# Denominators, softmax sums and gates spread by VectorE's 32x32 transposes instead of small transfers and broadcasts, phi(k) sums by additions, and another order

## The chip, the cores and the metric

The kernel runs on one core of one Trainium2 chip. The metric is the device time of one execution in microseconds. A profiled execution is taken beside the timed ones; its span runs from the first to the last instruction.

## The reference

Inputs are q, k and v of 8 batches x 8 heads x 576 positions x 64, and the weights. First comes linear attention, whose output, heads side by side, is the input x (576 x 512 per batch) of four causal attention experts of which each position uses two:

```python
def phi(x):
    proj = np.einsum('bhsd,df->bhsf', x, w_phi)
    proj = proj - np.max(np.abs(proj), axis=-1, keepdims=True)
    return np.concatenate([np.exp(proj), np.exp(-proj)], axis=-1)
q_p, k_p = (phi(q), phi(k))
kv = np.einsum('bhsf,bhsd->bhfd', k_p, v)
z = np.sum(k_p, axis=2)
num = np.einsum('bhsf,bhfd->bhsd', q_p, kv)
den = np.einsum('bhsf,bhf->bhs', q_p, z)[..., None] + 1e-06
x = num / den
...
logits = x @ w_gate          # gates: the 2 best of 4 experts, softmax over them
for e in range(4):
    q, k, v = x @ wq[e], x @ wk[e], x @ wv[e]
    a = causal_softmax(0.125 * (q @ k.T))
    out += gate[e] * (a @ v @ wo[e])
```

## The kernel before

**Staging.** Work goes by pairs of heads p (32 in all, four per batch) and, per batch b, by groups g of two experts (n = 2b+g, 16 in all). For a pair: `stream_k` projects k, `center` takes the maximum and subtracts it, ScalarE takes both exponentials into `ek`; `key_sum` sums `ek` over four blocks of positions into `zs` (28 of the 32 pairs); `stream_kv` multiplies `ek` with v and with ones and brings the result into `kv`. `stream_q` and `phi_q` do the same for q, with the maximum over partitions taken by GpSimd (`partition_all_reduce`), and leave the two halves of phi(q) in `mx` and `u`.

**Denominators.** `stream_n` computes a pair's denominators in two parts of positions (L633). `evac_d` copies them out of PSUM into rows of `dr`; four small transfers bring a row into 64 partitions x 9 numbers (`dc`), VectorE adds and inverts these (L665, L668), two transfers bring them back as rows, and GpSimd broadcasts the rows to the partitions of `xf` (L675, L677). Then the numerators (L643) are multiplied by `xf` in `divide` (L683), and the product is split into a high and a low part, xh and xl.

**Experts.** `stream_b` projects q and k of a group (`proj_t`), v and the gate logits of a batch (`proj_v`), then takes scores. `gates` computes the gate weights on VectorE (L822 to L840) into `gw` (the tile named col), transposes them on TensorE (L845) and sends them to DRAM. `mask` and `maxima` mask the scores and take the maximum over keys (GpSimd again, L885), L889 subtracts it, `expo` exponentiates. `sums` adds over keys with a matrix of ones (L919), copies the rows out into `max`, moves them by transfers to 64 x 9 (`sc`), inverts them, multiplies them with the gates read back from DRAM, moves them back and broadcasts them into `rb` (L947, L949). `attend` multiplies with v (L976), `evac_y` scales by `rb` (L988) and splits into yh and yl, `project_out` applies wo and `evac_o` stores.

**Order.** All DMAs are issued from SyncE's queue. The program order on each engine is fixed: a planner (`Plan`) runs the generators above as streams with a rank each (`POS`, `POS1`, `BOFF`, `NPOS`, `SLOPE`), estimates when each next step could start from written-down costs, and issues the step of best rank among those that can start soonest; copies out of PSUM go to ScalarE or VectorE by the same estimate. `in_order` then pins that order. TensorE works in three tilings (128x128, 64x128 and 128x32); eight PSUM tiles `c` are shared by all streams. Buffer counts: one `dr` (`DB`), one `rb` (`RB`), two `max` (`MB`).

Of the kernel before, what the change touches and what calls it, by code (L numbers as in the profile page):

```python
# [33 lines left out]
MB = 2  # L34
SUMJ = ()
SPLIT = 396
CACT = ()
TAILPE = True
RB = 1
DB = 1  # L40
PXB = 5
HOT = 1.08
SLOPE = (-6.05, 0.45, 3.02, 1.24, 1.41)
NPOS = (-8.38, 1.08)
UB = 4
FLEX = (5, -193)
# [5 lines left out]
ZEROS = 1.45  # L52

POS1 = {'k': -2.07, 'q': -0.65, 'v': 0.13, 'kv': 0.14, 'z': 0.36, 'cen': 0.7, 'evu': -4.26, 'ph0': 1.44, 'ph1': 0.38, 'div': 3.37, 'evd': -1.16, 'lk': -2.12, 'lq': -0.19}
BOFF = (0.83, 1.78, 1.5, 1.79, 1.95, 0.61, 1.44, 1.24)

ORDER = (('p0', 'v0', 's0', 'p1', 's1'), ('p0', 's0', 'p1', 's1', 'v0'))
POS = {'p0': 6.37, 'p1': -3.26, 'v0': 8.55, 'gate': 5.43, 's0': -1.94, 's1': 2.49, 'm0': 3.33, 'm1': 5.61, 't0': 5.6, 't1': 8.79, 'out': 13.84}
NPAIRS = B * NP
HEAD = 0.17  # L60
# [6 lines left out]
OTHER = 2.52  # L67
# [172 lines left out]
def tile_linear_attn_moe(ctx, tc, qt, kt, v, wts, out):  # L240
# [104 lines left out]
    drs = [sb(f"dr{i}", [128, S]) for i in range(DB)]  # L345
    dc = [sb(f"dc{i}", [128, 3, 9]) for i in range(2)]
# [6 lines left out]
    scs = [sb(f"sc{g}", [128, 9]) for g in range(2)]  # L353
# [118 lines left out]
    def key_sum(p, ek, ekk):  # L472
        for c in range(2):
            yield Step('DVE', ekk, pred=has('kv', p - 1) if p else None)
            dve(1024, ['zs'], ekk).tensor_reduce(out=zs[:, c], in_=ek[:, c, 0:8, :].rearrange("p (h a) f -> p h f a", h=2), axis=AX.X, op=ALU.add)  # L475
# [37 lines left out]
    def stream_kv():  # L513


        for p in range(NPAIRS):
# [6 lines left out]
            for t in range(NJ):  # L523
                for h in range(2):
                    u_ = 4 * h + t if t < 4 else 8
                    for k in range(2):
                        g = slice(64 * h + 32 * k, 64 * h + 32 * k + 32)
                        plan.run('PE', 256 / TRATE + 2, [kc], ekk + [vk], tiling=(128, 32))
                        nc.tensor.matmul(o[g, 0:2], v_in[:, 4 * h + t if t < 4 else 8 + h, 32 * k:32 * k + 32], ek[:, :, u_, :].rearrange("p c (w f) -> p c w f", w=4),  # L529
# [83 lines left out]
    def stream_n():  # L613


        for p in range(NPAIRS):
# [5 lines left out]
            def ready():  # L622
                return (all(('phi', p, h) in done for h in range(2)) and ('kvs', p) in done
                        and (p < DB or ('rb', p - DB) in done))

            for s0, s1 in PARTS:
                pk, ps = yield Step('PE', Pk + [kvk], 'c', ready, tiling=(128, 32)), rank(p) + NPOS[0]
                n = s1 - s0
                for h in range(2):
                    for c in range(2):  # L630
                        g = 64 * h + 32 * c
                        plan.run('PE', n / TRATE + 2, [pk], Pk + [kvk], tiling=(128, 32))
                        nc.tensor.matmul(ps[g:g + 32, 0:n], kvi[:, g // 32, 64:96], P_[h][c][:, s0:s1],  # L633
                                         start=True, stop=True, skip_group_check=True)
                plan.spawn(evac_d(p, s0, s1, pk, ps), rank(p) + POS1['evd'])
            for s0, s1 in PARTS:
                pk, ps = yield Step('PE', Pk + [kvk], 'c', has('rb', p), tiling=(128, 32)), rank(p) + NPOS[1]
                n = s1 - s0
                for c in range(2):
                    for h in range(2):  # L640
                        for g in range(64 * h, 64 * h + 64, 32):
# [6 lines left out]
    def evac_d(p, s0, s1, pk, ps):  # L648
# [6 lines left out]
        if not all(('dr', p, q_[0]) in done for q_ in PARTS):  # L655
            return
# [437 lines left out]
```

## Time and profile before

| | |
|---|---|
| median of 3 runs | 724.03 us (722.28 to 724.15) |
| the profiled execution's own time | 725.42 us |
| its span | 723.6 us |
| mean granted clock of TensorE | 0.964 |
| TensorE, VectorE, ScalarE, GpSimd busy | 663.6, 600.5, 399.8, 338.4 us |
| partition all-reduces of GpSimd (L604, L885) | 141.8 and 57.4 us |
| its four broadcast lines (L675, L677, L947, L949) | 30.9, 31.7, 14.1, 14.6 us |

Busy time is the union of an engine's instructions. A timeline row gives start, duration, engine, line, operation and count, and in brackets the idle time ahead and what ended it. A group's row gives busy time, mean duration in ns, and the idle time just before its members. A float32 matmul leaves two records, so counts of the trace are twice those of the program there.

### The profile page before, as it was taken

To read this page: it belongs to the slowest core of one execution; us is meant where nothing else is said; L and a number is where in the kernel's file an instruction comes from. 1 tells how busy PE (TensorE), PEld (TensorE's weight loads), DVE (VectorE), ACT (ScalarE), POOL (GpSimd) and SP (SyncE) were. 2 spreads that over 40 slices of the span, in tenths; PEclk is the share of its full clock that TensorE was granted. 3 is DMA by queue.
4 is the path that set the end of the run, shared out by engine and by line. 5 is a ranking of instruction groups with operands and counts; after the bars stand their busy time and mean duration, and the time that the engine had idled before them with its cause. 6 is when DMAs were issued, how large, how long until landed. Compare 5 with 4: busy or idle time off the path is not lost.

```text
span 723.6 us, 20271 instructions
## 1 busy us (share of the span) xinstructions
PE 663.6 (92%) x8058; PEld 505.2 (70%) x8058; DVE 600.5 (83%) x1155; ACT 399.8 (55%) x797; POOL 338.4 (47%) x263
## 2 busy tenths in 40 slices
PE   8989998899989999889988999998999899989984
PEld 6755668576786668555777777865787576858874
DVE  6888998979987889888998998897999985774742
ACT  4866656455756556435665755644576462463432
POOL 4635346643445554274336643375636631452420
PEclk9999999989999999999999999899999999999997
DMA  7642431123512152132421233222430221110011
GB/s 203 160 124 75 133 95 46 34 71 83 141 41 70 31 143 56 45 119 49 118 82 40 66 110 88 72 61 74 119 85 3 75 76 25 41 52 3 2 68 67
DMA packets 67007, 55.12 MB, mean 76 GB/s; under 512 B 43584, under 2 KB 49888, under 8 KB 66912
## 3 DMA queue, kind: packets, MB, share of 16 engines
q1 hardware_dynamic: 66912, 53.82, 27.0%
q8 instruction: 64, 1.05, 0.6%
q14 instruction: 31, 0.25, 0.1%
HBM read 38.16 MB, written 15.02 MB: 73 GB/s over the span
## 4 chain that ended last, share of the span: by engine, by line
PE 41%; DVE 24%; DMA 11%; SPq 9%; issue 8%; ACT 5%; POOL 2%; DVEq 0%; POOLq 0%; ACTq 0%
PE ps_c L265 13%; SPq L297 9%; PE ps_c L529 5%; PE ps_c L643 4%; PE ps_c L919 4%; PE ps_c L442 4%; DVE zs L475 4%; PE ps_c L770 4%; PE ps_c L976 3%; DMA dc<-dr 3%; PE ps_c L633 2%; DVE top L881 2%; DVE ek L502 2%; DMA ot<-in_wts_dram 2%; DVE pmax L488 2%
## 5 line engine op out<-in xcount | busy, mean ns | idle before, releaser
L604 POOL PARTITION_ALL_REDUCE mx<-u x64 | 141.8, 2258 | 115.9 <-ACT u L274 99.0
L475 DVE TENSOR_REDUCE zs<-ek 128x256 f32<-128x1024 f32 x56 | 110.3, 1986 | 3.5 <-PE ps_c L545 2.1
L265 PE MATMUL ps_c<-xh,qk 128*128 128x320 f32 (+1 forms) x512 | 108.7, 304 | 0.2
L276 ACT ACTIVATE ek<-ek 128x1152 f32<-128x1152 f32 x64 | 74.7, 1167 | 31.3 <-DVE ek L502 30.3
L265 PEld LDWEIGHTS ps_c<-xh,qk 128*128 128x128 f32 x512 | 85.1, 193 | 1.8 <-issue 0.6
L529 PE MATMUL ps_c<-ek,v_in 128*32 128x256 f32 x1280 | 80.9, 398 | 3.3 <-ACT ek L276 1.8
L868 POOL TENSOR_SCALAR_AFFINE_SELECT s<-s 128x256 f32<-128x256 f32 (+1 forms) x80 | 49.6, 652 | 71.3 <-ACT s L274 32.6
L885 POOL PARTITION_ALL_REDUCE max<-top x16 | 57.4, 3589 | 50.2 <-DVE top L881 15.0
L265 PE MATMUL ps_c<-xl,qk 128*128 128x256 f32 (+1 forms) x256 | 76.9, 300 | 0.6 <-DVE xl L269 0.6
L889 DVE TENSOR_TENSOR s<-s,max 128x1152 f32<-128x1152 f32 (+4 forms) x80 | 73.6, 955 | 1.1 <-POOL max L885 1.1
L276 ACT ACTIVATE s<-s 128x1152 f32<-128x1152 f32 (+4 forms) x80 | 55.5, 747 | 20.7 <-DVE s L889 19.5
L529 PEld LDWEIGHTS ps_c<-ek,v_in 128*32 128x32 f32 x1280 | 43.0, 114 | 33.6 <-issue 4.9
L265 PE MATMUL ps_c<-yh,wo 128*128 128x256 f32 (+1 forms) x256 | 56.6, 316 | 9.3 <-ACT yh L274 7.2
L675 POOL PARTITION_BROADCAST xf<-dr x32 | 30.9, 966 | 70.7 <-DMA dr<-dc 47.7
L265 PE MATMUL ps_c<-vg,xh 128*128 128x260 f32 (+1 forms) x320 | 59.8, 287 | 2.0 <-DVE rb L988 1.4
L442 PE MATMUL ps_c<-q_in,wf 64*128 64x256 f32 (+1 forms) x256 | 46.4, 434 | 10.7 <-ACT u L274 4.8
L606 DVE TENSOR_TENSOR u<-u,mx 128x576 f32<-128x576 f32 x64 | 53.5, 840 | 1.0 <-POOL mx L604 0.9
L276 ACT ACTIVATE mx<-u 128x576 f32<-128x576 f32 x64 | 43.6, 682 | 18.6 <-DVE u L606 18.4
L265 PEld LDWEIGHTS ps_c<-yh,wo 128*128 128x128 f32 x256 | 43.3, 201 | 13.2 <-ACT yh L274 7.5
L488 DVE TENSOR_REDUCE pmax<-ps_c 128x4 f32<-128x512 f32 (+1 forms) x96 | 50.2, 544 | 2.2 <-PE ps_c L442 2.2
L919 PE MATMUL ps_c<-s,ones 128*32 128x180 f32 (+5 forms) x576 | 48.7, 342 | 3.5 <-ACT s L276 2.9
L502 DVE TENSOR_TENSOR ek<-ps_c,pmax 128x512 f32<-128x512 f32 (+1 forms) x96 | 51.0, 547 | 0.1
(128 smaller groups left out, 1566.0 us busy)
## 6 DMA issues: line engine op xcount, KB each, us to landing
v_in<-in_v_dram SPq DMA_DIRECT2D x32, 320.0 KB
q_in<-in_qt_dram SPq DMA_DIRECT2D x64, 144.0 KB
out_dram<-ot SPq DMA_DIRECT2D x32, 288.0 KB
kvd<-kvt SPq DMA_DIRECT2D x112, 48.0 KB
kv<-kvd SPq DMA_DIRECT2D x28, 192.0 KB
k_in<-in_kt_dram SPq DMA_DIRECT2D x32, 160.0 KB
k_in<-in_kt_dram SPq DMA_DIRECT2D x32, 128.0 KB
dc<-dr SPq DMA_DIRECT2D x128, 2.2 KB
```

The lines of the kernel that those rows point to most:

```text
L265: nc.tensor.matmul(o, a, b, start=start, stop=stop, skip_group_check=True)
L276: nc.scalar.activation(o, i, func, **kw)
L297: nc.sync.dma_start(o, i)
L442: nc.tensor.matmul(o, a, b, start=True, stop=True, skip_group_check=True)
L475: dve(1024, ['zs'], ekk).tensor_reduce(out=zs[:, c], in_=ek[:, c, 0:8, :].rearrange("p (h a) f -> p h f a", h=2), axis=AX.X, op=ALU.add)
L488: dve(n * 128, [mk], [pk]).tensor_reduce(out=m[:, us], in_=src, axis=AX.X, op=ALU.max, apply_absolute_value=True)
L502: dve(n * 128, [e1k], [pk, mk]).tensor_tensor(out=ek2[p % EKB][:, 1, us, :], in0=src, in1=m[:, us].unsqueeze(2).to_broadcast([128, n, 128] ...
L529: nc.tensor.matmul(o[g, 0:2], v_in[:, 4 * h + t if t < 4 else 8 + h, 32 * k:32 * k + 32], ek[:, :, u_, :].rearrange("p c (w f) -> p c w f" ...
L604: nc.gpsimd.partition_all_reduce(M, U, 128, bass_isa.ReduceOp.absmax)
L885: nc.gpsimd.partition_all_reduce(big.rearrange("p e s -> p (e s)"), top.rearrange("p e s -> p (e s)"), 128, bass_isa.ReduceOp.max)
L889: dve(2 * (S - 128 * j), [('d', x, j)], [('max', z)], port=True).tensor_tensor(out=block(s_, j), in0=block(s_, j), in1=big[:, :, 128 * j:S ...
L919: nc.tensor.matmul(ps[r:r + 32, a - lo:z - lo], ones, src[:, e, a - c0:z - c0], start=first, stop=k == len(mine) - 1, skip_group_check=True)
```

## The change

In `key_sum`, two reductions per pair become three additions. In `stream_n` the two parts of the denominators become one PSUM tile of 32 equal rows per quarter: head h and every other block of 32 positions go to partitions 64*half + 32*h. The new helper `fractions` serves denominators and softmax sums: a 32x32-block transpose out of PSUM puts 32 positions on 32 partitions, so 9 columns hold all; these are inverted (and, for the sums, multiplied with the gates), copied to the other half of the partitions, widened to 576 columns and transposed again, which spreads each position's number over 32 partitions. `gates` no longer goes through DRAM: 16 small matmuls with pieces of the identity place the weights in `gc`. To fit the partitions, the columns of v, `vs` and the rows of the weights are taken in steps of two, and each weight piece is loaded in two halves. `dr`, `dc`, `sc`, `gtr`, `gd`, the 328 small transfers and 96 broadcasts are gone; `rb` gets two buffers, `max` one. The ranks and some of the planner's costs are other numbers, so every engine's order changes.

```diff
-MB = 2
-SUMJ = ()
-SPLIT = 396
+MB = 1
+NX = 1
-RB = 1
-DB = 1
+RB = 2
-NPOS = (-8.38, 1.08)
+NPOS = (-7.5, 3.69)
...
     def key_sum(p, ek, ekk):
-        for c in range(2):
-            yield Step('DVE', ekk, pred=has('kv', p - 1) if p else None)
-            dve(1024, ['zs'], ekk).tensor_reduce(out=zs[:, c], in_=ek[:, c, 0:8, :].rearrange("p (h a) f -> p h f a", h=2), axis=AX.X, op=ALU.add)
+        x = ek[:, :, 0:8, :].rearrange("p c (h a) f -> p c h a f", h=2)
+        for a in range(1, 4):
+            yield Step('DVE', ekk, pred=has('kv', p - 1) if p else None, port=True)
+            dve(512, ['zs'], ekk, 1.11, True).tensor_tensor(out=zs, in0=zs if a > 1 else x[:, :, :, 0], in1=x[:, :, :, a], op=ALU.add)
...
-    def evac_d(p, s0, s1, pk, ps):
...
+    def fractions(a, n, ps, pk, eps, out, wk, free, flag, gate=None):
+        i = n % NX
+        X, C, both = spreads[a][i]
+        key, bk = f'wide{a}{i}', f'both{a}{i}'
+        yield Step('DVE', [pk], pred=has('wide', a, n - NX) if n >= NX else None, hot=True)
+        dve(S // 2, [key], [pk], 1.13).transpose(X[:, 0:S // 2], ps[:, 0:S // 2])
+        plan.release('c', (pk, ps))
+        yield Step('DVE', [key], hot=True)
+        dve(9, [bk], [key]).tensor_scalar(out=C, in0=X[:, 0:S // 2:32], scalar1=eps, scalar2=None, op0=ALU.add)
+        halves = [(0, 0), (1, 1), (0, 1), (1, 0)]
+        if gate is None:
+            for src, dst in halves:
+                r, w = slice(64 * src, 64 * src + 64), slice(64 * dst, 64 * dst + 64)
+                yield Step('DVE', [bk], hot=True)
+                if src == dst:
+                    dve(9, [bk], [], 6.0).reciprocal(both[w, :, src], C[r])
+                else:
+                    dve(9, [bk], []).tensor_copy(both[w, :, src], both[r, :, src])
+        else:
+            yield Step('DVE', [bk], hot=True)
+            dve(9, [bk], [], 6.0).reciprocal(C, C)
+            for src, dst in halves:
+                r, w = slice(64 * src, 64 * src + 64), slice(64 * dst, 64 * dst + 64)
+                yield Step('DVE', [bk, 'gc'], pred=has('gate', n // 2), hot=True)
+                dve(9, [bk], ['gc']).tensor_tensor(out=both[w, :, src], in0=C[r], in1=gate[r], op=ALU.mult)
+            done.add(('gated', n))
+        st = Step((('ACT', 95 + 0.83 * S), ('DVE', 65 + 1.04 * S)), [bk], hot=True)
         yield st
+        copy(st.eng, S, X.rearrange("p (t i) -> p t i", i=32), both.rearrange("p a b -> p (a b)").unsqueeze(2).to_broadcast([128, 18, 32]), [key], [bk])
+        yield Step('DVE', [key], pred=free, hot=True)
+        dve(S, wk, [key], 1.13).transpose(out, X)
+        done.update((('wide', a, n), flag))
...
     def gates(b):
...
-        kc, ps = yield Step('PE', [G], 'c')
-        plan.run('PE', LDW, [kc], [G])
-        nc.tensor.transpose(ps[:, 0:128], gw, ident)
...
+        for g in range(2):
+            for a in range(2):
+                for half in range(2):
+                    for e in range(2):
+                        r, c = 64 * half + 32 * e, 64 * a + 32 * half
+                        nc.tensor.matmul(o[r:r + 32, g, :, a], ident[:, c:c + 32], gw[:, 5 * (2 * g + e):5 * (2 * g + e) + 5], start=True, stop=True, skip_group_check=True)
...
     def sums(n):
...
+        for j in range(NJ):
+            src = block(s_, j).rearrange("p e (a b i) -> p e b a i", b=2, i=32)
+            for half in range(2):
                 for e in range(2):
...
+                    nc.tensor.matmul(ps[r:r + 32, c0:S // 2].rearrange("p (a i) -> p a i", i=32), ones, src[:, e, half], start=j == 0, stop=j == NJ - 1, skip_group_check=True)
+        yield from fractions('y', n, ps, pk, 1e-9, rbs[y], [('rb', y)], has('ys', n - RB) if n >= RB else None, ('rb2', n), gc[:, g].rearrange("p j a -> p (j a)")[:, 0:9])
```

The order shows three places. First VectorE in the first batch, around the subtraction of the maxima of group 1 (tile s_153 before, s_156 after). Before:

```order
L286 COPY u_128<-ps_c_68 128x320
L665 SCALAR_TENSOR_TENSOR dc_141<-dc_141 128x9
L475 TENSOR_REDUCE zs<-ek_107 128x256
L668 RECIPROCAL dc_141<-dc_141 128x9
L475 TENSOR_REDUCE zs<-ek_107 128x256
L889 TENSOR_TENSOR s_153<-s_153,max_156 128x2x576
L937 TENSOR_SCALAR sc_158<-sc_158 128x9
L889 TENSOR_TENSOR s_153<-s_153,max_156 128x2x448
L939 RECIPROCAL sc_158<-sc_158 128x9
L889 TENSOR_TENSOR s_153<-s_153,max_156 128x2x320
```

Two reductions of phi(k) and the small work on dc and sc stand just ahead of and between the subtractions. After:

```order
L669 TENSOR_TENSOR bothy_144<-fewy_143,gc 64x9
L267 TENSOR_TENSOR xl_148<-xf,xh_147 128x320
L675 STREAM_TRANSPOSE xf<-wided_139 128x576
L669 TENSOR_TENSOR bothy_144<-fewy_143,gc 64x9
L681 TENSOR_TENSOR xf<-ps_c_64,xf 128x256
L681 TENSOR_TENSOR xf<-ps_c_63,xf 128x320
L562 STREAM_TRANSPOSE kvt<-ps_c_70 128x384
L675 STREAM_TRANSPOSE rb_159<-widey_142 128x576
L891 TENSOR_TENSOR s_156<-s_156,max_158 128x2x576
```

The reductions have moved away from there, and the last steps of both spreads stand in their place. Second, TensorE at the gates of the second batch (xh, xl and qk are the last q and k projections, ps_c a PSUM tile). Before:

```order
L265 MATMUL ps_c_66<-xh_146,qk 128x320
L265 MATMUL ps_c_66<-xl_147,qk 128x320
L265 MATMUL ps_c_66<-xh_146,qk 128x320
L845 MATMUL ps_c_68<-ident,col 128x128
L265 MATMUL ps_c_65<-yh_179,wo 128x256 x2
L265 MATMUL ps_c_65<-yl_180,wo 128x256
```

The transpose of the gates follows the projections at once. After:

```order
L263 MATMUL ps_c_66<-xh_149,qk 128x320
L263 MATMUL ps_c_66<-xl_150,qk 128x320
L263 MATMUL ps_c_66<-xh_149,qk 128x320
L527 MATMUL ps_c_63<-ek_107,v_in_105 32x2x4x32 x20
L849 MATMUL ps_c_68<-col,ident 32x5 x16
L543 MATMUL ps_c_63<-zs,ones 32x4x32 x4
```

Twenty matmuls of phi(k) with v now stand ahead of the gate matmuls; this is so in three batches of eight. Third, VectorE at the end of the program, from the last softmax sums on. Before:

```order
L937 TENSOR_SCALAR sc_159<-sc_159 128x9
L988 TENSOR_TENSOR rb_157<-ps_c_67,rb_157 128x256
L988 TENSOR_TENSOR rb_157<-ps_c_65,rb_157 128x320
L939 RECIPROCAL sc_159<-sc_159 128x9
L269 TENSOR_TENSOR yl_180<-rb_157,yh_179 128x256
L941 TENSOR_TENSOR sc_159<-sc_159,gc_176 128x9
L269 TENSOR_TENSOR yl_180<-rb_157,yh_179 128x320
L988 TENSOR_TENSOR rb_157<-ps_c_64,rb_157 128x256
```

Each of the three small operations on sc_159 waits for a transfer or for the other, and two broadcasts follow before the last row can run. After:

```order
L650 STREAM_TRANSPOSE widey_142<-ps_c_63 128x288
L954 TENSOR_TENSOR rb_159<-ps_c_64,rb_159 128x256
L653 TENSOR_SCALAR fewy_143<-widey_142 128x9
L665 RECIPROCAL fewy_143<-fewy_143 128x9
L669 TENSOR_TENSOR bothy_144<-fewy_143,gc 64x9
L267 TENSOR_TENSOR yl_177<-rb_159,yh_176 128x256
L669 TENSOR_TENSOR bothy_144<-fewy_143,gc 64x9 x3
L954 TENSOR_TENSOR rb_159<-ps_c_67,rb_159 128x320
L675 STREAM_TRANSPOSE rb_160<-widey_142 128x576
L267 TENSOR_TENSOR yl_177<-rb_159,yh_176 128x320
L954 TENSOR_TENSOR rb_160<-ps_c_68,rb_160 128x256
```

The whole chain now stands on VectorE, save one wide copy on ScalarE ahead of the last transpose.

More of the change, by code (lines that the diff above doesn't have):

```diff
@@ L66 @@
 PORT = 500.0
-OTHER = 2.52
+OTHER = 2.37
 LDW = 109.0
@@ L622, in ready @@
             def ready():
[L623 to L635, printed above, removed]
+                return all(('phi', p, h) in done for h in range(2)) and ('kvs', p) in done
+            pk, ps = yield Step('PE', Pk + [kvk], 'c', ready, tiling=(128, 32)), rank(p) + NPOS[0]
+            for c in range(2):
+                for half in range(2):
+                    for h in range(2):
+                        g = 64 * half + 32 * h
+                        plan.run('PE', S / 2 / TRATE + 2, [pk], Pk + [kvk], tiling=(128, 32))
+                        nc.tensor.matmul(ps[g:g + 32, 0:S // 2].rearrange("p (a i) -> p a i", i=32), kvi[:, 2 * h + c, 64:96],
+                                         P_[h][c].rearrange("p (a b i) -> p b a i", b=2, i=32)[:, half], start=c == 0, stop=c == 1, skip_group_check=True)
+            plan.spawn(fractions('d', p, ps, pk, 1e-6, xf, ['xf'], has('x', p - 1) if p else None, ('rb', p)), rank(p) + POS1['evd'])
             for s0, s1 in PARTS:
@@ L900, in sums @@
     def sums(n):
-        x, i, y = n % SB, n % MB, n % RB
+        x, y = n % SB, n % RB
         b, g = divmod(n, 2)
-        s_, top, rb, sc = ss[x], maxs[i], rbs[y], scs[g]
-        for j in SUMJ:
-            m = 2 * (S - 128 * j)
-            yield Step('DVE', [('P', x, 0), ('P', x, j), ('max', i)], port=True, pred=lambda: ('P', n, 0) in done and ('P', n, j) in done)
-            dve(m, [('max', i)], [('P', x, j)], port=True).tensor_tensor(
-                out=top[:, :, 128 * j:S], in0=block(s_, 0, 128) if j == 1 else top[:, :, 128 * j:S], in1=block(s_, j), op=ALU.add)
@@ L920, in sums @@
-        width = max(SPLIT, S - SPLIT)
-        st = Step(copies(width), [pk], hot=True)
-        yield st
-        srow = top[:, 0, 0:width]
-        copy(st.eng, width, srow, ps[:, 0:width], [('max', i)], [pk])
-        plan.release('c', (pk, ps))
-        for e in range(2):
-            for half, (lo, hi) in enumerate(((0, SPLIT), (SPLIT, S))):
-                r = 64 * e + 32 * half
-                yield Step('SP', [('max', i)])
-                load(sc[64 * e + lo // 9:64 * e + hi // 9, :], srow[r:r + 1, 0:hi - lo].rearrange("o (p c) -> o p c", c=9), ('sc', g, 2 * e + half), [('max', i)])
@@ L931, in sums @@
-        for e in range(2):
-            a = 640 * (2 * g + e)
-            yield Step('SP', [('gd', b % 2)], pred=has('gate', b))
-            load(gc[g][64 * e:64 * e + 64, :], gd[b % 2].rearrange("a b -> (a b)")[a:a + S].rearrange("(m c) -> m c", c=9), ('gc', g, e), [('gd', b % 2)])
-        sk, gk = [('sc', g, r) for r in range(4)], [('gc', g, e) for e in range(2)]
-        yield Step('DVE', sk)
-        dve(9, sk, []).tensor_scalar(out=sc, in0=sc, scalar1=1e-9, scalar2=None, op0=ALU.add)
-        yield Step('DVE', sk)
@@ L939, in sums @@
-        dve(9, sk, [], 8.0).reciprocal(sc, sc)
-        yield Step('DVE', sk + gk)
-        dve(9, sk, gk).tensor_tensor(out=sc, in0=sc, in1=gc[g], op=ALU.mult)
-        for e in range(2):
-            yield Step('SP', sk)
-            load(top[32 * e:32 * e + 1, 1, :].rearrange("o (m c) -> o m c", c=9), sc[64 * e:64 * e + 64, :], ('rs', i, e), sk + [('max', i)])
-        yield Step('POOL', [('rs', i, 0), ('rs', i, 1)], pred=has('ys', n - RB) if n >= RB else None)
-        plan.run('POOL', 1000, [('rb', y)], [('rs', i, 1), ('max', i)])
```

111 lines of the change are left out of this document (38 added, 73 removed).

## The prediction

> **What bounds the kernel now.** I read the page's totals first, then TensorE's stalls in the timeline, then what VectorE and GpSimd wait for, last the end of the program.
>
> ```profile
> span 723.6 us, 20271 instructions
> PE 663.6 (92%) x8058; PEld 505.2 (70%) x8058; DVE 600.5 (83%) x1155; ACT 399.8 (55%) x797; POOL 338.4 (47%) x263
> ...
> 0.00:80.00 80.00, 73.20 (x1015) 48.79 (x1018) 64.68 (x134) 53.43 (x94) 40.43 (x31) 0.96 0.52 140
> 80.00:690.00 610.00, 567.75 (x6815) 436.11 (x6808) 524.24 (x989) 336.24 (x680) 294.58 (x229) 0.97 0.25 68
> 690.00:723.60 33.60, 22.69 (x238) 20.26 (x236) 11.61 (x35) 10.16 (x24) 3.44 (x4) 0.89 0.20 73
> ```
>
> The last three rows are the busy times by stage (length, then PE, PEld, DVE, ACT, POOL, granted clock, DMA share, GB/s). TensorE sets the pace: it is busy 93% of the body (80 to 690 us), VectorE 86%. TensorE's work hardly changes here, so time can come only from its 42.3 us of idle in the body, from the 10.9 us in the last 33.6 us, and from clock. The large stalls in the body, of TensorE's own timeline, with what released each:
>
> ```profile
> 65.79 0.80 PE L442 MATMUL ps_c<-q_in,wf 64*128 64x320 f32 x2 [1.66 <-ACT dr L274]
> ...
> 146.33 1.71 PE L442 MATMUL ps_c<-q_in,wf 64*128 64x320 f32 x4 [4.14 <-ACT u L274]
> 176.66 0.51 PE L265 MATMUL ps_c<-vg,xh 128*128 128x260 f32 x2 [1.36 <-DVE rb L988]
> ...
> 236.49 0.70 PE L442 MATMUL ps_c<-q_in,wf 64*128 64x256 f32 x2 [1.88 <-DVE dr L286]
> ...
> 498.21 0.56 PE L265 MATMUL ps_c<-yh,wo 128*128 128x320 f32 x2 [2.15 <-DVE xf L683]
> 503.30 2.37 PE L529 MATMUL ps_c<-ek,v_in 128*32 128x256 f32 x40 [1.34 <-DVE max L286]
> ...
> 143.90:150.70 6.80, 4.37 (x22) 1.99 (x26) 5.30 (x14) 4.47 (x11) 4.00 (x4) 0.65 0.53 146
> ```
>
> These six sum to 12.5 us. The last row is the stage around the 4.14 us stall: clock 0.65, so a long stall is paid again in the matmuls behind it, 6.8 x 0.35 = 2.4 us there. Waits by pair (engine, line, what it waited for: us in total, times, longest):
>
> ```profile
> DVE sc L937 <- DMA sc<-max: 12.0, 6, 6.2
> DVE dc L665 <- DMA dc<-dr: 7.3, 8, 1.7
> DVE xf L683 <- POOL xf L677: 4.7, 3, 1.8
> DVE sc L941 <- DMA gc<-gd: 3.2, 4, 1.4
> DVE dr L286 <- DMA max<-sc: 2.6, 1, 2.6
> ...
> PE ps_c L845 <- DVE col L840: 12.3, 6, 3.2
> ...
> POOL xf L675 <- DMA dr<-dc: 47.7, 10, 12.1
> POOL rb L947 <- DMA max<-sc: 40.1, 8, 12.9
> ```
>
> The first five rows, 29.8 us, are VectorE standing still for the small transfers and broadcasts that the change takes out; the last two, 87.8 us, are GpSimd doing so.
>
> **The end of the program.** Here the transfers lie on the path:
>
> ```profile
> 698.01 0.28 PE L919 MATMUL ps_c<-s,ones 128*32 128x64 f32 x3
> ...
> 698.11 5.57 PE L976 MATMUL ps_c<-s,vs 128*32 128x256 f32 x109
> ...
> 709.91 0.86 POOL L949 PARTITION_BROADCAST rb<-max x1
> 710.80 0.82 DVE L988 TENSOR_TENSOR rb<-ps_c,rb 128x256 f32<-128x256 f32 x2 [4.02 <-POOL rb L949]
> ...
> 711.72 0.79 PE L265 MATMUL ps_c<-yh,wo 128*128 128x256 f32 x2 [5.02 <-ACT yh L274]
> ...
> 688.90:695.50 6.60, 6.60 (x50) 6.30 (x48) 1.00 0.24 91
> 711.70:720.00 8.30, 8.17 (x45) 7.90 (x45) 0.75 0.22 84
> ```
>
> The last sums end at 698.3, the products with v at 703.7, but the spread row is complete only at 710.8 and the output projection runs from 711.7, at clock 0.75: 45 matmuls in 8.17 us, where 50 took 6.60 at full clock (last two rows: L265 alone).
>
> **The change, part by part.** Prices come from these groups (busy us, mean ns), a tile's row (min/median/max ns), and two timeline rows:
>
> ```profile
> L475 DVE TENSOR_REDUCE zs<-ek 128x256 f32<-128x1024 f32 x56 | 110.3, 1986 | 3.5 <-PE ps_c L545 2.1 <-ACT ek L276 1.4
> L606 DVE TENSOR_TENSOR u<-u,mx 128x576 f32<-128x576 f32 x64 | 53.5, 840 | 1.0 <-POOL mx L604 0.9
> L564 DVE STREAM_TRANSPOSE kvt<-ps_c 128x384 f32<-128x384 f32 x28 | 16.1, 576 | 8.0 <-PE ps_c L545 7.1 <-ACT u L276 0.9
> L665 DVE SCALAR_TENSOR_TENSOR dc<-dc 128x9 f32<-128x9 f32 x32 | 12.9, 403 | 8.4 <-DMA dc<-dr 7.3 <-issue 0.9
> L838 DVE TENSOR_SCALAR gs<-gs 128x5 f32<-128x5 f32 x8 | 10.5, 1313 | 0.3
> L881 DVE TENSOR_TENSOR top<-top,s 128x384 f32<-128x384 f32 x16 | 9.9, 617 | 1.1
> L668 DVE RECIPROCAL dc<-dc 128x9 f32<-128x9 f32 x32 | 6.5, 204 | 0.0
> L937 DVE TENSOR_SCALAR sc<-sc 128x9 f32<-128x9 f32 x16 | 3.9, 243 | 12.0 <-DMA sc<-max 12.0
> L308 DVE STREAM_TRANSPOSE row<-col 128x32 f32<-128x32 f32 x1 | 0.2, 205 | 0.0
> ...
> L276 ACT ACTIVATE mx<-u 128x576 f32<-128x576 f32 x64 | 43.6, 682 | 18.6 <-DVE u L606 18.4
> ...
> L665 DVE SCALAR_TENSOR_TENSOR dc<-dc x32: 133/169/1839, 29.1 to 643.4; 128x9 f32<-128x9 f32 x32
> ...
> 28.26 1.06 PE L545 MATMUL ps_c<-ek,ones 128*32 128x128 f32 x32
> ...
> 693.77 0.30 PE L845 MATMUL ps_c<-ident,col 128*128 128x128 f32 x1
> ```
>
> **VectorE, sums of phi(k).** 56 reductions (110.3 us) become 84 additions of 128x512. Between the rows at 384 (617) and 576 (840) that size costs 766 ns: 64.3 us, 46.0 less. [...]
>
> **VectorE, spreading.** Out: the 9-wide work on dc (12.9+6.5) and sc (3.9, and 16 each at L668's and L665's prices, 3.3+6.4), 21 evacuations of the rows at 0.41 (half the 0.82 above), 8.6; and 25 other copies that the order now gives to ScalarE, 10.3. Together 51.9. In: the two transpose rows give 1.054 ns per column above 171 ns, so 48 of 288 columns cost 475 ns (22.8) and 48 of 576 cost 778 ns (37.3); 48 additions of the epsilon at 243 (11.7); 64 copies and 64 products at 0.30, between L937 and L665 (38.4; 31.1 to 51.6); 80 reciprocals at 204 (16.3); 8 of the 48 wide copies at about ScalarE's 682 (5.5). Together 132.0. VectorE is thus busy 600.5 - 46.0 - 51.9 + 132.0 = 634.6 us. With the waits on transfers and broadcasts it is occupied 630.3 us today; those go. I count VectorE as even: 0 on the path.
>
> **ScalarE** takes 40 wide copies (27.3 us), but loses 59 row copies and stays near 57%: hidden. *GpSimd* loses 96 broadcasts; it has 53% idle already, so its busy time is worth nothing by itself. *SP's queue* issues 381 transfers instead of 701: 328 small ones go, and 8 weight loads become 16 halves, early, before anything needs them (first use at 80 us): 0. The strided weights of v and vs change no instruction count; loads hide behind the matmuls (PEld 70%): 0.
>
> **TensorE.** Denominators and sums keep their columns (2x288 for 256+320 in each column group; 800 against at most 816). The 8 gate transposes (0.30 us each) become 8 groups of 16 matmuls of 5 columns, 32 records on the chip. The nearest row is L545's 32 records, 1.06 us: 8x0.76 = +6.1, from 0 (as cheap as today's) to +14 (2 us each). The order holds 234 changes of tiling instead of 219; an upper bound of 0.2 us each gives +3; I take +1.5.
>
> **Stalls in the body.** The six stalls stand at tiles that dr, max, rb or xf held, or (146.33) at a queue that two reductions of 2 us blocked: all rest on what is taken out. VectorE's new chain will hold tiles in its turn, so I let half go: -6.2 (0 to -12.5), and with them as much slow clock as in the stage shown, -2.4. At three of the gate places the order puts 20 matmuls of phi(k)v between the last q/k projection and the gate matmuls; the mean wait there was 12.3/6 = 2.05 us: -4 (0 to -6).
>
> **The end.** The new chain after the last sums: 0.48 + 0.24 + 0.20 + 4x0.30 + 0.68 + 0.78 = 3.6 us, with the hand-overs between engines some 4.5 (my estimate): ready at 702.8, before the products end at 703.7. From there the path 710.80 to 711.72 (0.92) gives a start at 704.7 instead of 711.7: -7.0. At full clock 45 matmuls take 5.94: -2.2. Together -9.2 (-5 if the chain is 4 us late, -11 at best).
>
> **Sum:** +6.1 + 1.5 - 6.2 - 2.4 - 4 - 9.2 = -14.2. GpSimd's queue, no longer blocked on transfers, brings the maxima earlier; for that I add -3 (0 to -15). The profiled execution took 725.4 us around its span of 723.6, 1.4 above the median of 724.0; 725.4 - 17.2 = 708.2, or 706.8 against the median. I predict 707.
>
> **The rivals.**
> **Slower: GpSimd holds up the new small operations.** L665 is 9 elements wide: median 169 ns, but up to 1839, mean 403; L838 has a mean of 1313. L668, right behind L665, never shows it. Such stretches come while GpSimd runs, and the change adds 176 operations of the kind that stretch. At 0.7 us each instead of the 0.29 priced, VectorE gains 72 us, to 707; with some 28 us that it idles at the two ends (22.0 of the last stage, the rest at the start) it becomes the bound, and the time is 735. It decides from about 0.63 us each (634.6 + 60 + 28 = 723). Against: 96 of GpSimd's instructions are gone, and most small ones sit between others. [...]
> **Much faster: GpSimd's queue was the hidden delay.** 87.8 us of its waits stood in front of the maxima that softmax and phi(q) need. If with them 20 more of the body's 42.3 us of idle go, and the clock of it, the time is 685 to 690. Against: most of GpSimd's waits end long before TensorE's work does.
> **No change: the transfers were hidden in the body.** A pair takes some 20 us and its chain 12, so only the end gains (-9.2), and gates, tilings and new waits in the new order (+8) give it back: 723.
>
> **How the numbers follow.** Forecast 0.50 (697 to 717), slower 0.19, much faster 0.20, no change 0.11. A measurement of this kernel tells 0.3%, 2.2 us, from no change. Faster: 0.50 + 0.20 + 0.04 of the last = 0.74; same 0.06; slower 0.19 + 0.01 = 0.20. The range 687 to 728 leaves out about half of each outer case.
>
> **What would show it.** Right: no wait on a small transfer on VectorE, output projection within 2 us of the last product with v, VectorE busy 615 to 650 us, additions near 0.75 us. Wrong: 9-element operations with means above 0.6 us; TensorE waiting at the gate matmuls longer than 12 us in all; gate groups above 2 us; new stalls behind the 288-column transposes. The order elsewhere, which I price only by its tilings, could also move the time either way.

## The result, and the profile after

The changed kernel takes 687.4 us (685.0 to 690.2), the kernel before 723.4 beside it: ratio 0.9505, 95% interval 0.9462 to 0.9549. That is 36 us faster, twice the forecast's 17; the direction was right and the time just inside the range's low end. The profiled execution took 685.0 us. Its totals:

```profile
span 683.2 us, 20283 instructions
...
PE 638.9 (94%) x8364; PEld 484.4 (71%) x8364; DVE 629.7 (92%) x1385; ACT 407.9 (60%) x803; POOL 248.9 (36%) x167
```

TensorE is busy 24.7 us less than before and idle 44.3 us (span minus busy) instead of 60.0; these two make up the difference of the spans, 40.4. (The spans differ by more than the medians, 36, because the profiled execution of the changed kernel was the fastest of its four and that of the kernel before, 725.4 us, was slower than its median.) The mean granted clock is 0.983 instead of 0.964. VectorE is busy 29.2 us more. By stage (length, PE, PEld, DVE, ACT, POOL, clock, DMA share, GB/s):

```profile
0.00:80.00 80.00, 75.04 (x1018) 52.32 (x1019) 70.32 (x164) 53.20 (x93) 34.57 (x23) 1.00 0.52 147
80.00:650.00 570.00, 534.43 (x6973) 406.83 (x6972) 538.27 (x1161) 339.24 (x675) 209.30 (x140) 0.98 0.24 70
650.00:683.30 33.30, 29.46 (x379) 25.28 (x377) 21.08 (x63) 15.47 (x37) 5.01 (x5) 1.00 0.19 72
```

The body's idle time fell from 42.3 to 35.6 us, that of the last 33 us from 10.9 to 3.8. The groups that answer to the priced rows (busy us, mean ns | idle before):

```profile
L473 DVE TENSOR_TENSOR zs<-zs,ek 128x512 f32<-128x512 f32 x56 | 40.0, 714 | 0.5
L914 PE MATMUL ps_c<-s,ones 128*32 128x288 f32 (+4 forms) x640 | 26.9, 313 | 0.1
...
L473 DVE TENSOR_TENSOR zs<-ek 128x512 f32<-128x512 f32 x28 | 18.8, 672 | 0.9 <-ACT ek L274 0.8
...
L662 DVE COPY bothd<-bothd 64x9 f32<-64x9 f32 x64 | 28.6, 447 | 1.8
...
L675 DVE STREAM_TRANSPOSE xf<-wided 128x576 f32<-128x576 f32 x32 | 24.7, 772 | 0.8
L669 DVE TENSOR_TENSOR bothy<-fewy,gc 64x9 f32<-64x9 f32 x64 | 22.2, 347 | 1.3
...
L650 DVE STREAM_TRANSPOSE wided<-ps_c 128x288 f32<-128x288 f32 x32 | 15.1, 473 | 3.5 <-PE ps_c L629 2.5 <-ACT s L274 0.5 <-ACT xh L272 0.3
...
L653 DVE TENSOR_SCALAR fewd<-wided 128x9 f32<-128x9 f32 x32 | 9.1, 285 | 0.1
...
L653 DVE TENSOR_SCALAR fewy<-widey 128x9 f32<-128x9 f32 x16 | 6.7, 420 | 0.2
...
L849 PE MATMUL ps_c<-col,ident 128*32 128x5 f32 x256 | 3.5, 176 | 5.6 <-DVE col L838 5.6
```

One row had no counterpart in the sum: the softmax sums on TensorE (L919 before, L914 now). Before, in the group table:

```profile
L919 PE MATMUL ps_c<-s,ones 128*32 128x180 f32 (+5 forms) x576 | 48.7, 342 | 3.5 <-ACT s L276 2.9 <-ACT u L274 0.5
```

The line lost 21.8 us, although it has 640 records now instead of 576, that is 40 instead of 36 in each of 16 groups. The largest waits of TensorE and VectorE that are left:

```profile
PE ps_c L543 <- DVE zs L473: 10.2, 10, 2.8
PE ps_c L629 <- DMA kv<-kvd: 5.7, 3, 3.9
PE ps_c L849 <- DVE col L838: 5.6, 4, 2.5
DVE ot L284 <- PE ps_c L263: 4.9, 2, 3.7
```

VectorE waits for no small transfer any more. TensorE's largest wait is for VectorE's phi(k) sums.

### The profile page after: what moved, and what is told of

Read it like the earlier page. It is cut to its first block, busy times and chain, and to the rows that moved or that the text cites. A ratio compares the mean times of both kernels' runs of the same rounds, so it can differ in the third digit from the quotient of the medians.

```text
span 683.2 us, 20283 instructions
## 1 busy us (share of the span) xinstructions
PE 638.9 (94%) x8364; PEld 484.4 (71%) x8364; DVE 629.7 (92%) x1385; ACT 407.9 (60%) x803; POOL 248.9 (36%) x167
## 5 line engine op out<-in xcount | busy, mean ns | idle before, releaser
L274 ACT ACTIVATE ek<-ek 128x1152 f32<-128x1152 f32 x64 | 74.6, 1166 | 28.3 <-DVE ek L500 24.7
L527 PE MATMUL ps_c<-ek,v_in 128*32 128x256 f32 x1280 | 77.3, 387 | 2.7 <-DVE xf L681 2.3
L891 DVE TENSOR_TENSOR s<-s,max 128x1152 f32<-128x1152 f32 (+4 forms) x80 | 68.6, 887 | 0.5 <-POOL max L887 0.3
L527 PEld LDWEIGHTS ps_c<-ek,v_in 128*32 128x32 f32 x1280 | 39.6, 112 | 28.8 <-issue 2.8
L263 PE MATMUL ps_c<-yh,wo 128*128 128x256 f32 (+1 forms) x256 | 54.5, 308 | 0.4 <-ACT ot L272 0.4
L272 ACT COPY wided<-bothd 128x576 f32<-128x576 f32 x27 | 18.1, 672 | 60.2 <-DVE bothd L662 60.2
L272 ACT COPY s<-ps_c 128x512 f32<-128x512 f32 (+1 forms) x98 | 43.4, 535 | 16.4 <-PE ps_c L768 16.4
L604 DVE TENSOR_TENSOR u<-u,mx 128x576 f32<-128x576 f32 x64 | 50.8, 804 | 0.0
L263 PEld LDWEIGHTS ps_c<-xl,qk 128*128 128x128 f32 x256 | 49.7, 194 | 0.0
L263 PEld LDWEIGHTS ps_c<-vg,xh 128*128 128x128 f32 (+1 forms) x320 | 47.3, 178 | 1.9 <-DVE wided L650 1.0
```

The costliest lines, as they stand in the source:

```text
L263: nc.tensor.matmul(o, a, b, start=start, stop=stop, skip_group_check=True)
L272: nc.scalar.copy(o, i)
L274: nc.scalar.activation(o, i, func, **kw)
L604: dve(S, [uk], [mk], port=True).tensor_tensor(out=U, in0=U, in1=M, op=ALU.subtract)
L891: dve(2 * (S - 128 * j), [('d', x, j)], [('max', z)], 1.11, True).tensor_tensor(out=block(s_, j), in0=block(s_, j), in1=big[:, :, 128 * j: ...
```

## The experiments

Ratios are to the kernel before, run beside each; busy times are those of the profiled run.

| kernel | us | ratio (95%) | PE busy | DVE busy |
|---|---|---|---|---|
| after | 687.4 | 0.9505 (0.9462 to 0.9549) | 638.9 | 629.7 |
| before, sums side by side | 720.3 | 0.9913 (0.9884 to 0.9942) | 653.0 | 602.6 |
| before, additions | 705.7 | 0.9718 (0.9654 to 0.9782) | 655.7 | 567.0 |
| before, new numbers of the order | 717.8 | 0.9869 (0.9829 to 0.9908) | 660.1 | 600.8 |
| before, all three (no spreading) | 690.7 | 0.9513 (0.9470 to 0.9556) | 644.5 | 564.5 |
| after, sums half first | 693.6 | 0.9544 (0.9509 to 0.9580) | 655.1 | 630.2 |
| after, reductions, new order | 735.6 | 1.0127 (1.0096 to 1.0158) | 661.4 | 679.4 |
| after, reductions, same order | 734.2 | 1.0120 (1.0083 to 1.0157) | 659.4 | 678.6 |
| after, old numbers of the order | 719.8 | 0.9916 (0.9885 to 0.9946) | 648.6 | 644.2 |
| after, one transfer in each chain | 754.3 | 1.0387 (1.0338 to 1.0437) | 666.2 | 623.7 |
| after, reciprocals for copies | 675.5 | 0.9309 (0.9268 to 0.9350) | 632.3 | 618.9 |
| after, crossing copies on ScalarE | 661.0 | 0.9120 (0.9085 to 0.9156) | 627.2 | 605.4 |
| the last, small additions there too | 660.2 | 0.9108 (0.9069 to 0.9147) | 626.4 | 599.9 |

### The softmax sums' loop, turned in both kernels

In the kernel before:

```diff
-        for half, (lo, hi) in enumerate(((0, SPLIT), (SPLIT, S))):
-            ...
-            for k, (src, c0, a, z, first) in enumerate(mine):
+        ...
+        for k, half, lo, count, src, c0, a, z, first in sorted(both, key=lambda m: m[0:2]):
                 for e in range(2):
```

> The kernel before with one loop turned: the softmax sums' matmuls alternate between the two halves of the columns instead of finishing one half first. The same 36 matmuls of the same sizes a group; every other instruction of every engine keeps its place. Theory A (only matmuls that stand next to each other and go to different groups of 32 columns run side by side; half-outermost used two of the four groups): one group of sums falls from 2.68 us to about 1.5 to 1.6, the line's busy time from 48.7 to 26 to 30 us, and, since TensorE is busy 92% of the span, the kernel by 15 to 20 us, to 703 to 708. Rival B (the sums are cover: what they leave free turns into waits for VectorE, GpSimd or transfers): the groups shorten but the time falls by under 5 us. Rival C (the sums cost the same in either order, and the changed kernel's cheaper groups come from its 288-column strided rows): 2.68 us stays, 723.

In the changed kernel:

```diff
-        for j in range(NJ):
-            for half in range(2):
+        for half in range(2):
+            for j in range(NJ):
                 for e in range(2):
```

> The changed kernel with one loop turned back: in the softmax sums the half is outermost again, as before; 40 matmuls a group of the same sizes, everything else in its place. Theory A: a group rises from 1.57 us to about 2.7, the line from 26.9 to about 45 us, and the kernel by 14 to 19 us, to 701 to 706, near the 707 that was predicted with this term at nothing. Rival B: the line rises, the time by under 5 us. Rival C: no change, 687.

One group in TensorE's timeline, of before, of before with the loop turned (32 of its 36 records; the other four follow among the next matmuls and end 1.8 us after the start), of after, of after with the loop turned back (start, duration):

```profile
683.31 2.68 PE L919 MATMUL ps_c<-s,ones 128*32 128x396 f32 x36
```
```profile
692.82 1.68 PE L921 MATMUL ps_c<-s,ones 128*32 128x396 f32 x32
```
```profile
656.88 1.57 PE L914 MATMUL ps_c<-s,ones 128*32 128x288 f32 x40
```
```profile
662.32 2.73 PE L914 MATMUL ps_c<-s,ones 128*32 128x288 f32 x40
```

The same matmuls cost 2.7 us when one half of the columns comes first, and 1.6 to 1.8 when the halves alternate. That fits theory A: in these groups, matmuls whose neighbours go to other groups of 32 columns of the array ran side by side. By their starts, four records of the changed kernel's group begin within 0.02 us and the next four 0.27 us after the first; in the kernel before, two begin within 0.01 us and the next two 0.36 us after the first. With the half outermost, neighbours used two of the four groups, and the columns of both halves (816 + 784) came one after the other. The gain is a factor of 1.5 (before) and 1.7 (after), not the 2 of perfectly shared halves. Rival C is out. The line's busy time moved by 16.4 and 19.0 us (48.7 to 32.3; 26.9 to 45.9), close to theory A, but the kernel only by 6.3 us one way (0.87% of 724) and by 3 (ratios, whose intervals overlap) to 6 us (medians) the other. TensorE's idle time took part of it: 66.6 us instead of 60.0 in the kernel before, 35.9 instead of 44.3 in the changed one. The kernel gets well under half of what this line is spared, so theory A's 15 to 20 us, and its 14 to 19 the other way, missed; rival B's under 5 us came nearer.

### The additions, alone and undone

The kernel before with additions, in its own order:

```diff
         for c in range(2):
             yield Step('DVE', ekk, ...)
-            dve(1024, ['zs'], ekk).tensor_reduce(out=zs[:, c], ...)
+            plan.run('DVE', 65 + 1.04 * 1024, ['zs'], ekk)
+            for a in ((1,), (2, 3))[c]:
+                nc.vector.tensor_tensor(out=zs, in0=zs if a > 1 else x[:, :, :, 0], in1=x[:, :, :, a], op=ALU.add)
```

> The kernel before with the phi(k) sums as three additions of 512 elements instead of two reductions; the planner still counts the reductions, so all other instructions keep their places. VectorE's busy time falls by about 51 us, to 550. Theory A (VectorE's work is on the path wherever TensorE waits for zs or for ek behind it, in the kernel before too): 690 to 708. Rival B (in the kernel before, the transfers' waits leave VectorE slack, so that the additions only pay once these waits are gone): 719 to 726, which is the 0 that the prediction gave this part.

The changed kernel with the two reductions again, first with an order laid out for them, then in the same order as with additions:

```diff
-        for a in range(1, 4):
-            ...(out=zs, in0=zs if a > 1 else x[:, :, :, 0], in1=x[:, :, :, a], op=ALU.add)
+        for c in range(2):
+            dve(1024, ['zs'], ekk).tensor_reduce(out=zs[:, c], ...)
```

> The changed kernel with the phi(k) sums as two reductions again (about 110 us on VectorE for 56, where 84 additions took 58.8). Theory A (VectorE at 92% has become the second bound, so its 52 us saved were needed): VectorE's busy time rises to about 681 us and the kernel by 15 to 35 us, to 702 to 722. Rival B (VectorE's share is off the path, as the prediction counted it: 0): VectorE rises but the time by under 4 us. The planner lays out the order anew for the new durations, so a few us of either sign can come from that.

```diff
         for a in range(1, 4):
             ...
+            if a != 2:
+                c = a // 2
+                nc.vector.tensor_reduce(out=zs[:, c], ...)
```

> The changed kernel with the two reductions instead of the three additions, the planner still counting the additions, so that all other instructions keep their places (the run with reductions and a new order took 735.6). VectorE rises by about 51 us. Theory A (VectorE itself is the bound once it holds the spreading too): 725 to 745. Rival B (the 48 us came from the order that the planner laid out for the longer durations): 690 to 705.

The additions alone give the kernel before 2.8%, 20 us of 724. Without them the changed kernel loses 48 us in a new order and 47 in the same one: it is VectorE's work, not the order, and without them the whole change would be slower than before. Theory A's mechanism holds in all three; the run with reductions and a new order lost more than the 15 to 35 us it gave. In the kernel before, VectorE's busy time fell by 33.5 us, not by the 51 expected: the 84 additions take 813 ns on average there (68.3 us), 685 ns with GpSimd at rest, 907 beside one of its broadcasts and 957 beside an all-reduce. The page of before had phi(k)'s sums in its chain that ended last, the work followed back from the last instruction (shares of the span, by engine and by line):

```profile
PE 41%; DVE 24%; DMA 11%; SPq 9%; issue 8%; ACT 5%; POOL 2%; DVEq 0%; POOLq 0%; ACTq 0%
PE ps_c L265 13%; SPq L297 9%; PE ps_c L529 5%; PE ps_c L643 4%; PE ps_c L919 4%; PE ps_c L442 4%; DVE zs L475 4%; PE ps_c L770 4%; PE ps_c L976 3%; DMA dc<-dr 3%; PE ps_c L633 2%; DVE top L881 2%; DVE ek L502 2%; DMA ot<-in_wts_dram 2%; DVE pmax L488 2%
```

VectorE's zs is its largest line there, 27.5 us (3.8% of the span). The engines' row of the kernel before with additions, and both rows of the changed kernel with reductions in the changed kernel's order:

```profile
PE 49%; DVE 9%; issue 4%; DMA 4%; SPq 2%; ACT 2%; POOL 1%; POOLq 0%; DVEq 0%; ACTq 0%
```
```profile
DVE 54%; PE 31%; ACT 5%; issue 4%; DMA 3%; SPq 2%; DVEq 0%; ACTq 0%
PE ps_c L263 13%; DVE zs L476 11%; DVE ek L503 5%; DVE pmax L489 4%; PE ps_c L643 4%; DVE s L894 4%; PE ps_c L771 3%; PE ps_c L439 3%; DVE u L607 3%; DVE xl L267 3%; DVE bothd L665 2%; DVE top L886 2%; DVE xf L684 2%; DVE xf L678 2%; PE ps_c L945 2%
```

The chain of the kernel before with additions could be followed back over 71% of the span only (its shares add up to 71), so VectorE has 13% of what was followed; in the last 71% of the span of before it has 25%, about what it has in the whole. With additions VectorE's share thus falls to about half; with the spreading and without the additions it is 54%, and zs alone 11%. The changed kernel's own chain reaches back over 38% only, of which TensorE has 18 and VectorE 16.

### The numbers of the order

```diff
-SLOPE = (-6.05, 0.45, 3.02, 1.24, 1.41)
+SLOPE = (-11.47, 0.23, -2.41, -1.03, 0.53)
... (and NPOS, FLEX, ZEROS, POS1, BOFF, POS, HEAD, OTHER)
```

> The kernel before with only the changed kernel's numbers of the order (SLOPE, NPOS, FLEX, ZEROS, POS1, BOFF, POS, HEAD, OTHER). Theory A (the numbers fit their own kernel's durations, and are worth nothing by themselves): same to slower, 723 to 750, with the softmax sums' line still at 47 to 50 us. Rival B (the other order is what made the gain beyond the forecast): 700 to 712.

The other way, the old numbers in the changed kernel:

> The changed kernel with the numbers of the order that the kernel before has (SLOPE, NPOS, FLEX, ZEROS, POS1, BOFF, POS, HEAD, OTHER); buffers and code as changed. Theory A (the numbers are worth to the changed kernel about what they were worth to the kernel before, 8 us): 691 to 699. Rival B (the new numbers fit only the new code, whose VectorE has little slack): 700 to 725. Rival C (worth nothing here): 685 to 690.

Both theories of the first missed: the numbers give the kernel before 1.3%, 9.5 us. The changed kernel needs them far more: with the old ones it takes 719.8, 32 us more, as its rival B had it, and VectorE's busy time rises to 644.2. Why they are worth three times as much there was not taken apart.

### Everything but the spreading

The kernel before with the loop turned, the new numbers and the changed kernel's `key_sum`, whose additions the planner now counts; denominators, sums and gates still go by transfers and broadcasts, and the buffer counts are those of before.

> The kernel before with everything of the change but the spreading: the phi(k) additions, the sums' matmuls side by side, and the changed kernel's numbers of the order; the denominators, softmax sums and gates still travel by small transfers and GpSimd's broadcasts. Theory A (the parts add up: 6, 19 and 8 us were measured for each alone): 689 to 695, and the spreading would be worth only 2 to 8 us in the changed kernel. Rival B (the parts share their gain, or the numbers need the spreading): 696 to 712, and the spreading is worth 9 to 25. Rival C (the spreading costs): under 686.

Theory A: 690.7. The three ratios multiply to 0.9913 x 0.9718 x 0.9869 = 0.9507, measured together 0.9513, and the changed kernel, with the spreading, has 0.9505. In this order the part that names this change thus adds nothing that can be told from nothing (the intervals are half a per cent to each side). With the old numbers it would cost: loop and additions alone multiply to 0.9633, and the changed kernel with the old numbers has 0.9916, about 20 us more (an estimate; no run has loop, additions and old numbers together). It is not that the spreading does nothing. The end, in this kernel without the spreading and in the changed one (busy by stage as above, then TensorE's wait):

```profile
670.00:689.40 19.40, 9.51 (x48) 8.95 (x48) 4.57 (x11) 4.07 (x10) 2.29 (x3) 0.70 0.17 63
```
```profile
PE ps_c L265 <- ACT yh L274: 9.0, 2, 5.6
```
```profile
664.00:683.30 19.30, 15.46 (x212) 12.02 (x211) 9.59 (x27) 6.84 (x17) 0.00 (x0) 1.00 0.29 109
```

Without it the output projection still waits 9.0 us and runs at a clock of 0.70; with it there is no such wait and full clock. From the end of the last product with v to the end of the span, the kernel without the spreading takes 23.0 us and the changed one 10.7. But it reaches that product's end at 666.4 us, and the changed one only at 672.5; up to there TensorE idles 31.4 us without the spreading and 40.5 with it. So the gain at the end is real, and something ahead of it pays most of it back. VectorE is busy 564.5 us without the spreading and 629.7 with it; the experiments below take some of that work off it.

### One transfer back in each chain

```diff
         dve(9, [bk], [key]).tensor_scalar(out=C, ...)
+        nc.sync.dma_start(late, C)
...
-                    dve(9, [bk], [], 6.0).reciprocal(both[w, :, src], C[r])
+                    dve(9, [bk], [], 6.0).reciprocal(both[w, :, src], late[r])
```

> The changed kernel with one small transfer put back into each of the 48 spreads: the 128x9 sums go through SyncE's queue into another buffer of the same shape before the reciprocals (a 128x9 transfer took 2.2 us from issue to landing in the kernel before, two of them stood in each chain there, with four to six issues). The planner is told nothing, so all other instructions keep their places. Theory A (VectorE, in order, now stands still for each transfer): its 48 waits of some 2 to 2.5 us, partly under work that waits anyway, make 40 to 110 us: 725 to 795. Rival B (the chain is hidden behind TensorE's other work, as the rival 'no change' had it): 686 to 695.

```profile
DVE bothd L661 <- DMA lated<-fewd: 48.1, 31, 3.6
DVE fewy L666 <- DMA latey<-fewy: 24.2, 16, 3.3
```

VectorE stands still 72.3 us in 47 waits, and the kernel is 67 us slower: theory A. TensorE idles 87.7 us instead of 44.3, and its matmuls take 27.3 us longer, at a mean clock of 0.948 instead of 0.983. Where the order puts no other work between, these waits on VectorE cost nearly their length, so this order needs a chain without transfers. The kernel before, whose order was laid out for them, waited 29.8 us on transfers and broadcasts in all, with two transfers in each chain. The expectation's 2.2 us is a misreading: the view of before gives 2.2 KB for these transfers and no time (the chain of before that ended last holds eight of dc<-dr, at 1.9 to 3.9 us). The transfers put in here took 1.7 us (median) from issue to landing.

### What GpSimd does to the small operations

The 0.30 us priced for the 9-wide copies and products came out at 0.40 ((28.6 + 22.2) / 128). The tile's rows say how (min/median/max ns):

```profile
L660 DVE RECIPROCAL bothd<-fewd x64: 166/210/214, 31.0 to 616.1; 64x9 f32<-64x9 f32 x64
L662 DVE COPY bothd<-bothd x64: 157/170/1390, 33.2 to 618.2; 64x9 f32<-64x9 f32 x64
```

and two such copies in VectorE's timeline, with what GpSimd does at the time:

```profile
202.46 0.17 DVE L662 COPY bothd<-bothd 64x9 f32<-64x9 f32 x1
202.66 0.48 DVE L650 STREAM_TRANSPOSE widey<-ps_c 128x288 f32<-128x288 f32 x1
203.17 1.26 DVE L662 COPY bothd<-bothd 64x9 f32<-64x9 f32 x1
```
```profile
203.11 2.14 POOL L602 PARTITION_ALL_REDUCE mx<-u  x1 [5.16 <-ACT u L272]
```

Of the 176 small additions, copies and products, the 70 that overlap an all-reduce of GpSimd take 710 ns on average, the 103 that overlap nothing 160 (none over 174), three that overlap a select 166. The 80 reciprocals take 204 on average with GpSimd at rest and 206 beside an all-reduce. The next kernel reads the reciprocals for the other half from the sums instead of copying them:

```diff
-                    dve(9, [bk], []).tensor_copy(both[w, :, src], both[r, :, src])
+                    dve(9, [bk], []).reciprocal(both[w, :, src], C[r])
```

> The changed kernel with the 64 copies that carry a denominator's reciprocals to the other half of the partitions (on VectorE, 168 ns each while GpSimd runs nothing, 744 ns mean in the 31 that overlap a GpSimd instruction) turned into reciprocals of the same 64x9 elements, read from the sums themselves (203 and 206 ns in the same trace). All instructions keep their places. Theory A (GpSimd holds VectorE's copies, additions and products, but not its reciprocals): VectorE's busy time falls by 64 x 0.24 = 15 us, and the kernel by 5 to 12 us, to 675 to 682. Rival B (the hold moves to the next copy or addition): VectorE falls by under 5 us, the time by under 3. Rival C (the length of VectorE's work does not matter here; the run with ScalarE gained from its new order): VectorE falls by 15, the time stays at 685 to 689.

```profile
L662 DVE RECIPROCAL bothd<-fewd x64: 203/209/213, 33.8 to 608.7; 64x9 f32<-64x9 f32 x64
```

12 us faster, the same order, from 64 small instructions. VectorE's busy time fell by 10.8 us, not 15: a part of the hold moved on to the additions behind (zs<-zs,ek 44.1 us instead of 40.0). Theory A, with some of rival B in it.

Next, the crossing copies go to ScalarE:

> The changed kernel with the 9-element copies or products that cross from one half of the partitions to the other (two of each spread, 96 in all) as copies on ScalarE instead of VectorE; the planner orders anew. VectorE's busy time falls by about 96 x 0.41 = 39 us if these cost their mean there. Theory A (VectorE is the second bound in the changed kernel): 672 to 682. Rival B (ScalarE's step makes the chain from the denominators to their spread rows longer, and the numbers of the order no longer fit): 686 to 697. Rival C (VectorE no longer bounds at 630): 685 to 689.

```diff
                 else:
-                    yield Step('DVE', [bk], hot=True)
-                    dve(9, [bk], []).tensor_copy(both[w, :, src], both[r, :, src])
+                    yield Step('ACT', [bk], hot=True)
+                    act(9, both[w, :, src], both[r, :, src], [bk], [bk])
```

and the same for the products' other half. 661.0 us, 26 below the changed kernel and below theory A's 672 to 682. VectorE is busy 24.3 us less, not the 39 expected, and the copies cost ScalarE 0.20 us each, whatever GpSimd does (64 of the 96, none over 203 ns):

```profile
L272 ACT COPY bothd<-bothd x64: 199/200/203, 32.4 to 592.1; 64x9 f32<-64x9 f32 x64
```

The order is new here, so not all of the 26 us need be VectorE's. The last kernel moves the additions of the small constant as well:

```diff
-        yield Step('DVE', [key], hot=True)
-        dve(9, [bk], [key]).tensor_scalar(out=C, in0=X[:, 0:S // 2:32], scalar1=eps, scalar2=None, op0=ALU.add)
+        yield Step('ACT', [key], hot=True)
+        act(9, C, X[:, 0:S // 2:32], [bk], [key], AF.Copy, bias=eps)
```

> The version with the crossing copies on ScalarE (661.0 us), and also the 48 additions of the small constant (128x9, 188 and 319 ns mean there, 11.1 us in all) on ScalarE as copies with a bias; the planner orders anew. Theory A (VectorE's work, and above all what GpSimd can hold, is what TensorE waits for): VectorE falls by 8 to 11 us, the time by 4 to 9, to 652 to 657. Rival B (at 95% TensorE is the bound and another hop to ScalarE and back only lengthens the chain, by some 0.4 us in each of 48): 660 to 670.

660.2 us: VectorE fell by 5.5 us more (8 to 11 were expected) and the time did not follow (0.9108 against 0.9120). The time is rival B's. TensorE is busy 95% of the span in both. These two are the fastest versions, 8.8 and 8.9% below the kernel before.

## Why the prediction was right or wrong

**VectorE, "I count VectorE as even: 0 on the path": this step failed, and it holds the largest error.** Its busy time was nearly right (629.7 against 634.6), but the two parts do not lie on the path alike: the additions alone are worth 20 us, and the spreading puts 65 us of work on VectorE that eats the gain at the end (without 64 of its copies the kernel is 12 us faster). The prediction read the totals and TensorE's stalls, and not the chain, where zs stood with 3.8%. TensorE's stalls name the last releaser only; a reduction that had held that releaser up does not appear there.

**TensorE, "Denominators and sums keep their columns": failed.** It assumed that the sums used all four column groups before ("800 against at most 816"). They used two at a time. The line fell by 21.8 us; turning that loop alone gives 6 us.

**Other order**, priced by tilings (+1.5) and the place of the gates (-4) only: its numbers are worth 9.5 us to the kernel before. (The prediction's 0.2 us for a change of tiling stands on no row that it shows; where TensorE does not wait, the first matmul after a change of tiling starts 0.21 us after the one ahead, median in both traces, so the tilings' term was not the miss.) The prediction named the rest of the order as open; it gave it no term.

**Stalls in the body, -6.2 and -2.4, because "all rest on what is taken out": not so.** The body's idle time did fall by 6.7 us, gates included. But up to the end of the last product with v TensorE idles 49.1 us before, 40.5 in the changed kernel and 31.4 in the kernel without the spreading, which still has the transfers. So what the additions, the loop and the order did was put down to the transfers, and taking these out went with more idle time there, not less.

**Gates, +6.1 and -4.** A group of 32 records takes 0.44 us (3.5 / 8), near the old transposes' 0.30 and not L545's 1.06: +1.1 in all. The wait fell from 12.3 to 5.6 us, 6.7, a little over the range's end of 6. At the three places with 20 matmuls of phi(k)v ahead TensorE still waits 0.6, 0.2 and 2.3 us, at a fourth without them 2.6. As priced, this gain is the order's and not the spreading's: with the old transposes and the new numbers alone TensorE waits 6.5 us there, with loop and additions besides 4.6.

**The end, -9.2: right in mechanism and size.** The last sums end at 667.1, the products at 672.5, and wo follows at once at full clock. From the end of the products to the end of the span it is 10.7 us instead of 19.9, 9.2 less. The kernel without the spreading still takes 23.0, so this term is the spreading's.

**GpSimd's queue, -3, and the rival "much faster" (685 to 690).** The time came out as that rival had it, but not by its mechanism: the kernel with the transfers and broadcasts, whose GpSimd still waits 82.0 us for dr alone, takes 690.7.

**The slower rival** was right that GpSimd holds the small operations, but not by as much as its 0.7 us each: the 176 have a mean of 0.38 us ((28.6 + 22.2 + 9.1 + 6.7) / 176), between the priced 0.29 and the 0.63 at which it would have decided. It erred on the point from which the hold costs anything: VectorE need not be the bound for its work to count. Removing 64 of these copies gained 12 us at 92%. Beside an all-reduce the 64x9 copies took 744 ns on average and the products 573, where they took 168 and 159 with GpSimd at rest; the reciprocals took 206 and 204. The phi(k) additions took 862 ns beside an all-reduce and 676 alone, where the reductions before took 1984 and 1983. Why some are held and others are not, no run shows. The copy shown above ended at 204.43 us, ahead of the all-reduce beside it, which by its row ran to 205.25.

**Durations:** the additions took 700 ns on average (58.8 us), where the two rows gave 766. The transposes (473 and 772 ns against 475 and 778) and reciprocals were right.

The prediction's four signs of being right all came true: VectorE waits on no small transfer, the output projection follows the last product at once, VectorE is busy 629.7 us (615 to 650 was the sign), and the additions take 0.70 us. They tell what the new parts cost and not what the gain rests on, and so could not tell this forecast from its rivals. The forecast's sign came right by luck: it rested on the parts of the spreading, whose sum, measured as one in the new order, is nothing, and the gain came from three parts, two of them counted at 0 and the order by a few of its places only.

## What to carry to other kernels

When a change comes in parts, price each part against the chain of work that ended last as well as against busy shares: an engine at 83% beside one at 92% gave 20 us for 33 us of work, because both take turns on the chain. See first how much of the span a chain covers: some here reach back over 38 or 71% only. On TensorE, put neighbouring matmuls into different column groups before changing anything else (here a group of sums went from 2.68 to 1.8 us by that alone, and the kernel gained 6 us). Give small operations that stand beside GpSimd's reductions a form that these did not hold here (a reciprocal instead of a copy, 206 ns beside an all-reduce instead of 744, or a copy on ScalarE, 199 to 203).

## What the runs showed of the hardware

- A group of softmax sums (36 or 40 records of matmuls that fill 32 of the array's 128 columns) took 2.7 us with neighbours in two of the four column groups, and 1.6 to 1.8 us with all four in turn. The issue order alone moved the time, in both kernels.
- VectorE's 64x9 copies took 168 ns with GpSimd at rest and 744 on average, up to 1390, beside its all-reduces; reciprocals of the same size 203 and 207 on average (the changed kernel), and 64 of ScalarE's copies 199 to 203 whatever GpSimd did.
- VectorE's 128x512 additions took 685 ns with GpSimd at rest, 907 beside its broadcasts and 957 beside its all-reduces (averages, the kernel before with additions); the reductions that they replace took 1983, 1997 and 1984.
